# RetNet recurrence with a SwiGLU block: k's second layout made on TensorE for two chunks, q's decay table spread from two rows, four integer sums on GpSimd, and another order of the first steps

## The chip, the cores and the metric

The kernel runs on one core of a Trainium2 chip. The metric is the time of one execution in device microseconds (us). The core has TensorE (PE; PEld is its loading of weights), VectorE (DVE), ScalarE (ACT), GpSimd (POOL) and SyncE (SP), which here only issues DMA transfers. Each engine works through its own list of instructions in order and waits on semaphores for the others.

## The reference

```python
batch, n_heads, seq, head_dim = (4, 8, 768, 64)
gamma = 1.0 - 2.0 ** (-5.0 - np.arange(H))
for t in range(S):
    state = gamma * state + np.einsum('bhd,bhe->bhde', k[:, :, t], v[:, :, t])
    y[:, :, t] = scale * np.einsum('bhd,bhde->bhe', q[:, :, t], state)
x = y.transpose(0, 2, 1, 3).reshape(B * S, H * D)      # 3072 tokens x 512
g = x @ w_gate                                         # 512 x 1536
out = (g / (1 + np.exp(-g)) * (x @ w_val)) @ w_out     # 1536 x 512
```

q, k and v are float32. The three weights are float64, which the kernel reads as pairs of 32-bit words.

## The kernel before

**The work.** The sequence is cut into chunks of 128 steps, six for each of the four batch entries. Within a chunk the recurrence is a masked product: scores of k and q (`scores`, L628), times a decay mask on VectorE (L634), times v (`mix`, L713). From chunk to chunk a state of 64x64 a head is carried: `state` (L684) adds k scaled by its decay times v, `decay` (L670) shrinks the old one, and `mix_old` (L699) adds q, scaled by its own decay, times the state. The result x goes through the two weights (`plain_part` L906, `plain` L888, in later segments `product` L1057) and the third (`down`, L1126). Products of the second part are done with each operand split into three parts, made by ScalarE, VectorE and GpSimd in turn.

**Segments.** Six chunks make a segment (768 tokens), and there are four. The first segment's chunks 0 to 5 are handled one after the other at the start of the program, while the weights are read from HBM for the first time and turned from float64 into float32; only this start differs between the two kernels.

**The order** is written out by hand in the string `PLAN`. Of each entry the letter is the step, the number the chunk or piece, and what follows a colon a part of it: `s` scores, `m` mix, `o` mix_old, `t` state, `g` decay of the state, `x` splitting the result into parts (L969, L976, L399), `k`/`K` scaling k on GpSimd or VectorE (L649), `q`/`Q` scaling q (L643), `l3:1` loading for chunk 3 its piece 1 (pieces are k^T, q^T, v, k; called k, q, v and k_n here), `A` loading a third of the table of decays, `U` and `V` loading a piece of weights, `a`, `b`, `c`, `S`, `C` converting it (ScalarE L532, L535, L538; VectorE L545; sum L553 or L555), `n` splitting a weight (L960, L963, L966), `p`, `v`, `u`, `y` the first plain products and what follows them, `T` and `Z` making sums of a weight and writing it back, `h` and `L` small tables for later. `run` issues them in this order, so PLAN fixes the order on every engine.

**Two layouts of k.** The scores take k with the 64 elements of a head down the partitions; the state takes it with the 128 steps down the partitions. Both are loaded from HBM (`l0:0` and `l0:3` for chunk 0), as arrays laid out beforehand.

**Tables.** `tab` holds for each partition the masks (1024 columns), q's decay (512 columns, `qdec`), k's decay (8 columns, `kdec`) and the state's (4 columns). It is loaded in three slices, `A0`, `A1` (the masks) and `A2` (all the rest).

**Weights in halves.** The first two pieces of the first weights are converted half by half (`a0:0`, `a0:1` and so on). The low word is scaled by ScalarE (L538), the sign bits by ScalarE and VectorE (L535, L545), and an integer sum of both closes it (L553 on VectorE). For pieces of the third weight that sum is on GpSimd (L555).

**DMA.** All loads at the start but two (q of chunks 0 and 1, issued by ScalarE) are issued by SyncE in order. Eight semaphores are used in turn for all of them, so a load is issued when the one eight before it has landed.

Of the kernel before, what the change touches and what calls it, by code (L numbers as in the profile page):

```python
# [14 lines left out]
AF = mybir.ActivationFunctionType  # L15
ALU = mybir.AluOpType

P = 128
# [32 lines left out]
    l0:0 l1:0 A0 A1 s0 U0:0 l0:2 l0:3 a0:1 s1 b0:1 A2 h0 S0:1 m0 K0 x0:2 c0:1 l2:0 x0:1 l2:1 l1:3  # L51
    C0:1 t0 l1:2 V0:0 l3:1 n0:0 s2 a0:0 Q2 l3:0 l2:3 n0:1 b0:0 S0:0 m1 k1 x1:1 x1:2 l2:2 c0:0 n0:2
    U1:1 C0:0 t1 o2 l3:3 g2 s3 n0:3 n0:4 l4:1 p0:0 m2 a1:1 x2:1 k2 q3 b1:1 l4:0 a1:0 x2:2 S1:1 l5:1
    l3:2 n0:5 c1:1 k3 t2 C1:1 o3 b1:0 l5:0 l4:2 g3 v0:0 s4 S1:0 t3 l5:2 c1:0 C1:0 U2:0 m3 s5 U12:3
    U3:1 q5 q4 u0:0 a2 o5 o4 T0:0 n1:0 m4 b2 y0:0 x3:1 x3:2 m5 T0:1 n1:1 n1:3 T0:2 S2 n1:2 p0:1 v0:1
    n1:4 T1:0 x4:1 u0:1 y0:1 a12 n1:5 x5:1 U4:0 T1:1 a3 p1:0 x4:2 u1:0 p1:1 x5:2 Z0 u1:1 T1:2 c12
    v1:0 U5:1 y1:0 v1:1 p0:2 Z1 l5:3 v0:2 c2 C2 b12 y1:1 p1:2 n2:0 a4 U6:0 u0:2 b3 n2:1 u1:2 v1:2
    S12 n2:3 L y0:2 S3 c3 n2:2 U13:2 G2:0 n2:4 T2:0 G2:1 C3 y1:2 T2:1 n3:0 b4 n2:5 n3:1 i2:0 i2:1
    T2:2 W2:0 j2:0 n3:2 W2:1 G3:1 n3:3 S4 C12 a5 Z2 j2:1 Z12 n3:4 c4 C4 U7:1 n3:5 T3:0 T3:1 c13 T3:2
    G3:0 n4:0 n4:1 b5 S5 n4:2 W3:0 n4:3 W3:1 i3:0 i3:1 n4:4 a13 a6 G4:1 c5 Z3 b13 G4:0 T4:0 U8:0 C5  # L60
    T4:1 j3:1 n4:5 b6 U14:3 W4:1 n5:0 T4:2 n5:1 i4:1 n5:2 n5:3 j3:0 S6 i4:0 a7 c6 n5:4 W4:0 T5:0 C6
    G5:1 Z4 T5:1 n6:0 U9:1 j4:0 n5:5 S13 G5:0 a8 b7 n6:3 T5:2 j4:1 n6:1 c14 C13 W5:1 S7 i5:1 Z5 n6:4
# [12 lines left out]
    1/y0.05 T10:1 1/was0.1 1/y0.15 1/y0.00 1/y0.14 0/d2.1 0/D1.4 1/y0.12 0/d2.2 0/D1.2 1/y0.13 0/W3
    Z17 0/D1.3 0/Z2 0/d3.0 0/D1.0 0/h2.2 0/h3.1 1/C0 0/W4 T10:2 0/h3.2 0/d3.1 0/h4.2 Z10 1/y0.16
    1/l7 1/y0.17 1/new0.1 1/sum0.0 0/D2.3 0/D2.1 1/y0.10 0/h5.0 1/begin 1/sum0.1 0/d3.2 0/h5.1
    1/y0.11 0/D2.5 1/sc1 0/D2.0 0/d4.0 1/was1.0 0/D2.4 0/d4.1 0/D3.4 1/l6 1/dec1.1 0/h5.2 1/dec1.0
    0/D2.2 1/x0.2.0 0/D3.1 1/q1.1 0/d4.2 0/W5 0/D3.5 1/x0.1.0 0/h6.0 1/k1.0 0/Z3 1/sum0.3 1/k1.1
    1/sum0.2 1/x0.2.1 0/D4.5 0/D3.2 0/D3.3 0/D3.0 1/q1.0 0/Z4 0/h6.1 0/D4.0 0/D4.4 1/x0.1.2 1/x0.1.1  # L80
    1/A1 1/x0.0.0 0/d5.0 1/x0.2.2 1/y1.00 0/h6.2 1/y1.06 1/x0.0.2 1/new1.0 0/D4.2 0/d5.1 0/d5.2
    0/D4.3 0/D4.1 1/y1.07 1/y1.01 0/W6 0/h7.0 1/B1 1/x0.0.1 1/y1.04 1/y1.12 0/h7.1 1/l9 0/d6.0
    0/D5.4 0/h8.0 0/d6.1 1/y1.02 0/D5.3 0/D5.2 0/W7 0/h8.1 1/y1.05 0/d6.2 1/l8 1/l11 0/Z5 1/y1.03
    1/was1.1 0/D5.5 1/C1 0/d7.0 1/y1.16 0/d7.1 0/D6.5 0/D5.0 1/y1.17 1/y1.15 1/new1.1 0/h7.2 1/y1.14
    1/y1.11 0/D5.1 1/y1.13 1/x1.2.0 0/D6.3 0/d7.2 0/D6.4 0/Z6 1/y1.10 0/D7.3 0/h9.0 1/sc2 0/h8.2
    1/x1.2.2 0/D6.2 1/q2.1 1/k2.1 0/D7.5 0/W8 1/sum1.0 0/D6.1 1/sum1.2 1/k2.0 0/D6.0 0/D7.1 1/x1.1.0
    0/h10.0 0/h9.1 0/d8.0 0/D7.2 1/dec2.0 1/l10 1/sum1.1 1/dec2.1 0/W9 1/x1.1.1 0/D7.0 0/d8.1
    1/x1.2.1 0/Z7 1/sum1.3 1/was2.0 1/q2.0 1/x1.0.0 1/x1.1.2 0/d9.0 0/D7.4 0/d8.2 0/h11.0 1/A2
    1/new2.0 0/D8.0 1/x1.0.1 0/h10.1 0/D8.3 0/D8.2 0/d9.1 1/L0 0/D8.1 1/y2.00 0/D8.4 1/B2 0/W10
    0/d9.2 1/y2.07 1/y2.05 0/d10.0 0/D8.5 0/h9.2 1/y2.02 0/h11.1 0/D9.3 1/y2.03 0/h10.2 1/y2.01  # L90
    0/D9.5 0/Z8 1/y2.04 1/y2.06 1/w0.0.0 0/D9.4 0/d10.1 0/h11.2 1/C2 1/y2.16 1/y2.14 0/W11 1/y2.12
    0/D9.1 1/y2.10 0/D9.2 1/L1 0/d10.2 0/D10.3 0/Z9 0/d11.0 1/y2.17 1/x1.0.2 1/y2.15 1/y2.13 0/D9.0
    1/L2 0/D10.4 0/D10.1 1/sum2.2 0/D10.2 0/D10.0 1/y2.11 0/d11.1 1/sum2.0 0/d11.2 1/x2.1.0 1/sum2.1
    1/x2.1.2 1/sum2.3 0/D11.1 0/Z11 1/w0.1.0 0/D11.0 1/x2.0.0 0/D11.3 0/D10.5 0/D11.4 1/w0.0.1
    0/D11.2 1/w0.0.2 1/w1.0.0 1/x2.1.1 1/x2.0.1 0/Z10 1/w1.0.1 0/e0 1/x2.0.2 1/w1.0.2 0/D11.5 1/p0.0
    1/u0.0 1/p0.1 1/p0.2 1/p1.0 1/x2.2.0 1/u0.1 1/w0.2.0 0/e2 1/x2.2.1 1/w0.1.1 1/p1.1 1/x2.2.2 0/e1
    1/w0.1.2 0/e3 1/w1.2.0 1/w1.1.0 1/w0.2.1 1/u1.0 1/w2.1.0 1/u0.3 1/p1.2 1/w1.1.1 1/p0.3 1/u0.4
    1/p0.4 1/w0.2.2 1/u0.5 1/p0.5 1/u0.6 1/w1.2.1 1/w2.0.0 1/w1.1.2 1/u1.3 1/p0.6 1/u0.8 1/p1.3
    1/w2.0.1 1/p1.4 1/u1.4 1/w2.0.2 1/u1.1 1/L3 1/u0.9 1/p1.5 1/p2.0 1/w2.2.0 1/w1.2.2 1/u1.5
    1/w3.2.0 1/u0.2 1/w2.1.1 1/w3.2.1 1/u1.2 1/w3.1.0 1/u1.6 1/u2.0 1/w3.0.0 1/w3.0.1 1/p1.6  # L100
    1/w2.1.2 1/p2.1 1/p2.3 1/w3.1.1 1/L4 1/p2.2 1/u1.8 1/u2.4 1/u2.1 1/u2.3 1/p2.5 1/w3.0.2 1/w4.2.0
    1/u1.9 1/u2.6 1/w2.2.1 1/p2.4 1/w3.2.2 1/L5 1/p3.1 1/w2.2.2 1/u2.5 1/u1.7 1/w4.1.0 1/w4.0.0
    1/u0.7 1/p3.0 1/u3.0 1/w3.1.2 1/w4.0.1 1/w4.1.1 1/p2.6 1/p3.2 1/u3.3 1/p3.3 1/p3.4 1/u3.4 1/u2.2
    1/u2.8 1/p3.5 1/u3.1 1/u3.5 1/L6 1/w5.1.0 1/p3.6 1/w4.0.2 1/u2.9 1/w4.1.2 1/u3.6 1/w5.0.0
    1/w4.2.1 1/p4.1 1/w5.0.1 1/p4.0 0/e5 2/begin 1/w5.2.0 1/w5.0.2 1/u3.8 1/p4.3 1/u4.0 1/w5.1.1
    1/u4.4 1/u3.9 1/w5.2.1 1/p4.2 1/u4.3 1/L7 1/u3.2 1/w5.1.2 1/p4.5 1/p5.0 1/u4.1 1/p4.4 1/u4.5
    1/w6.1.0 1/p5.1 1/u5.0 1/w4.2.2 1/w6.0.0 1/w6.1.1 1/p5.2 1/u5.1 1/u4.6 0/e4 1/w6.1.2 1/u2.7
    1/w6.0.1 1/w6.2.0 1/w5.2.2 1/u5.3 1/p4.6 1/p5.3 1/p5.4 1/u5.4 1/u4.8 1/p5.5 1/u5.5 1/L8 1/w7.2.0
    1/p5.6 1/u4.9 1/w6.0.2 1/u4.2 1/w7.1.0 1/w8.2.0 1/p6.1 1/u5.6 1/w7.0.0 1/u4.7 1/w7.2.1 1/p6.0
    1/u3.7 1/w7.1.1 1/w7.0.1 1/u6.0 1/w8.2.1 1/u5.2 1/u6.1 1/L10 1/p6.3 1/w7.0.2 1/u6.4 1/u5.8  # L110
# [1198 lines left out]
```

## Time and profile before

| what | value |
|---|---|
| median of three runs | 642.8 us (642.61 to 645.92) |
| the profiled execution | 642.91 us |
| its span, first to last instruction | 641.1 us |
| TensorE busy | 631.2 us, 98% |
| DMA share in 24.18:32.02 us | 1.06 of 16 engines, 373 GB/s |

The page's slices show how TensorE and the DMA engines are filled over the span, each digit a fortieth (16 us) and in tenths:

```profile
PE   6999999999999999999999999999999999999997
...
DMA  9998978689887445258775540467777444304554
```

Reading: TensorE is short of work in the first slice and at the very end only. The chain that ended last runs over TensorE for 94% of the span and over DMA transfers for 4%:

```profile
PE 94%; DMA 4%; ACT 0%; DVE 0%; SPq 0%; issue 0%; ACTq 0%
```

### The profile page before, as it was taken

What the parts mean: (1) busy time and instruction counts of PE and PEld (TensorE: products, weight loads), DVE (VectorE), ACT (ScalarE), POOL (GpSimd) and SP (SyncE); (2) the same over time, 40 slices, a digit from 0 to 9 for tenths busy, and PEclk for the clock granted to TensorE, in tenths of its full rate; (3) what the DMA queues carried; (4) which work ended last, traced back from release to release, by engine and by line L of the source; (5) the groups of instructions that cost most, each with busy time, mean ns of one, the idle gap of its engine ahead of it and who ended that gap; (6) DMA issues with size and microseconds to landing.
All of it is one profiled execution on the core that took longest, in us unless ns stands there. A gap on an engine that the chain in (4) does not pass through costs nothing.

```text
span 641.1 us, 14110 instructions
## 1 busy us (share of the span) xinstructions
PE 631.2 (98%) x5579; PEld 579.5 (90%) x5579; DVE 485.6 (76%) x713; ACT 392.2 (61%) x860; POOL 265.4 (41%) x174
## 2 busy tenths in 40 slices
PE   6999999999999999999999999999999999999997
PEld 6899999988779999997778999998777999999886
DVE  5887888999898887665787869675789866768351
ACT  3687697777865565566766555564785555654221
POOL 0535455544427865630002665550101666663000
PEclk9999999999999999999999999999999999999999
DMA  9998978689887445258775540467777444304554
GB/s 322 375 359 295 356 264 301 267 306 319 269 278 290 168 148 173 73 180 260 246 240 214 199 160 10 183 196 243 228 240 263 157 164 172 116 0 153 193 184 178
DMA packets 50626, 140.13 MB, mean 219 GB/s; under 512 B 4992, under 2 KB 17792, under 8 KB 50560
## 3 DMA queue, kind: packets, MB, share of 16 engines
q1 hardware_dynamic: 49984, 138.44, 62.8%
q8 instruction: 44, 0.72, 0.5%
q10 hardware_dynamic: 576, 0.79, 0.3%
q14 instruction: 22, 0.18, 0.1%
HBM read 109.32 MB, written 29.88 MB: 217 GB/s over the span
## 4 chain that ended last, share of the span: by engine, by line
PE 94%; DMA 4%; ACT 0%; DVE 0%; SPq 0%; issue 0%; ACTq 0%
PE bank L1057 41%; PE bank L1126 31%; PE bank L888 13%; PE bank L758 6%; PE bank L906 2%; DMA rawp<-in_w_gate_dram 1%; DMA oitem<-wdnt 1%; DMA hT<-in_k_n_dram 1%; DMA hT<-in_q_t_dram 1%; PE bank L713 0%; PE bank L684 0%; PE bank L699 0%; PE bank L628 0%; SPq L464 0%; DVE bank L545 0%
## 5 line engine op out<-in xcount | busy, mean ns | idle before, releaser
L1126 PE MATMUL bank<-oitem,gitem 128*128 128x512 f32 x867 | 208.4, 394 | 0.5 <-DMA oitem<-wdnt 0.3
L1126 PEld LDWEIGHTS bank<-oitem,gitem 128*128 128x128 f32 x867 | 159.6, 188 | 35.2 <-DMA oitem<-wdnt 0.7
L966 POOL TENSOR_TENSOR gitem<-gitem 128x768 fp32r<-128x768 f32 x72 | 142.0, 1982 | 115.3 <-DVE gitem L963 96.3
L1057 PE MATMUL bank<-xa,gitem 128*128 128x384 f32 x864 | 160.5, 334 | 0.0
L1057 PEld LDWEIGHTS bank<-xa,gitem 128*128 128x128 f32 x864 | 150.8, 188 | 0.2
L966 POOL TENSOR_TENSOR oitem<-oitem 128x256 fp32r<-128x256 f32 (+1 forms) x60 | 65.9, 1106 | 53.7 <-DVE oitem L963 53.3
L1057 PE MATMUL bank<-xb,gitem 128*128 128x384 f32 x432 | 84.5, 334 | 0.0
L888 PE MATMUL bank<-xa,oitem 128*128 128x384 f32 x480 | 84.2, 335 | 0.0
L963 DVE SCALAR_TENSOR_TENSOR gitem<-gitem,loads 128x768 fp32r<-128x768 f32 x72 | 76.0, 1070 | 9.9 <-ACT gitem L960 8.4
L888 PEld LDWEIGHTS bank<-xa,oitem 128*128 128x128 f32 x480 | 83.0, 188 | 0.2
L1057 PEld LDWEIGHTS bank<-xb,gitem 128*128 128x128 f32 x432 | 75.9, 188 | 0.4
L960 ACT ACTIVATE gitem<-loads 128x768 fp32r<-128x768 f32 x72 | 59.6, 843 | 26.0 <-PE bank L1057 16.8
L963 DVE SCALAR_TENSOR_TENSOR gitem<-gitem,hT 128x768 fp32r<-128x768 f32 x48 | 46.2, 965 | 26.1 <-ACT gitem L960 26.1
L960 ACT ACTIVATE gitem<-hT 128x768 fp32r<-128x768 f32 x48 | 40.2, 842 | 32.8 <-PE bank L1126 30.7
L991 ACT COPY chunk_x<-bank 64x128 f32<-64x128 f32 x144 | 36.6, 260 | 31.8 <-PE bank L758 21.2
L399 DVE SCALAR_TENSOR_TENSOR gitem<-gitem 128x768 fp32r<-128x768 f32 x48 | 48.8, 1025 | 0.8
L785 POOL TENSOR_TENSOR loads<-loads,tab 128x512 f32<-128x512 f32 x9 | 13.3, 1479 | 81.8 <-PE bank L758 58.4
L1057 PE MATMUL bank<-xb,oitem 128*128 128x384 f32 x216 | 43.4, 335 | 0.0
L1057 PEld LDWEIGHTS bank<-xb,oitem 128*128 128x128 f32 x216 | 37.9, 188 | 0.3
L1074 DVE TENSOR_TENSOR hT<-bank,tmp 128x384 f32<-128x384 f32 x36 | 20.0, 555 | 20.4 <-PE bank L1057 20.2
L1072 ACT COPY tmp<-bank 128x384 f32<-128x384 f32 x36 | 17.2, 478 | 28.3 <-PE bank L1057 19.3
L963 DVE SCALAR_TENSOR_TENSOR oitem<-oitem,loads 128x256 fp32r<-128x256 f32 (+1 forms) x42 | 33.8, 808 | 0.9 <-ACT oitem L960 0.8
(114 smaller groups left out, 785.7 us busy)
## 6 DMA issues: line engine op xcount, KB each, us to landing
loads<-wup SPq DMA_DIRECT2D x36, 896.0 KB, 4.6
oitem<-wdnt SPq DMA_DIRECT2D x33, 768.0 KB, 4.4
wdnt<-oitem SPq DMA_DIRECT2D x12, 768.0 KB, 6.1
wup<-first SPq DMA_DIRECT2D x9, 896.0 KB, 6.0
rawp<-in_w_gate_dram SPq DMA_DIRECT2D x12, 512.0 KB, 7.2
rawp<-in_w_val_dram SPq DMA_DIRECT2D x12, 512.0 KB, 6.3
rawp<-in_w_out_dram SPq DMA_DIRECT2D x12, 512.0 KB, 7.3
out_dram<-chunk_x SPq DMA_DIRECT2D x21, 256.0 KB, 2.2
```

The costliest lines, as they stand in the source:

```text
L399: stt(o, x, 1.0, y, op0=mul, op1=op)
L758: nc.tensor.matmul(o, a, b, start=start, stop=True, skip_group_check=True)
L785: (pool if i else both)(t, t, qdec, op=mul)
L888: nc.tensor.matmul(o, w[:, a, ts(b, P)], X0[:, a, i, NC - 1 - b], start=a == b == 0, stop=a == 2 and b == NC - 1, skip_group_check=True)
L960: act(o[0], x, AF.Copy, scale=CUT / FAR)
L963: stt(o[1], f32(o[0]), -FAR, x, op0=mul, op1=add)
L966: op(o[2], f32(o[0]), f32(o[1]), op=add)
L991: copy(cx[half[i], ds(2 * h, 2), c, half[z]], y.rearrange("p (b t) -> p b t", b=2))
L1057: nc.tensor.matmul(o, w[:, a, k], x[:, a, KH - 1 - k], start=start and a == k == 0, stop=a == 2 and k == KH - 1, skip_group_check=True)
L1072: steps = (lambda: copy(p1, x), lambda: tt(c11, z, p1, op=add), lambda: act(gate, c11, AF.Silu, scale=ONE), lambda: copy(u2, x), lambda: c ...
L1074: lambda: copy(p5, wb), lambda: tt(h1, x, p5, op=add),
L1126: nc.tensor.matmul(banks[tok][:, cols], hs[f][:, a, ds(i * TH + u * P, P)], wo[f][:, a, cols], start=f == a == 0, stop=f == NF - 1 and a = ...
```

## The change

Eight things are other than before, all in the start:

- k_n of chunks 0 and 1 is not loaded (`l0:3`, `l1:3` gone). `r0` and `r1` make it on TensorE: k^T of each pair of heads is taken as weights against a unit matrix (`unit_of`, step `I`, made of the mask's diagonal on VectorE), four matmuls 128x128 by 128 columns into bank 2 or 3.
- k of chunk 0 is scaled on VectorE as before (`K0`), now from bank 2; k of chunk 1 by ScalarE in eight pieces from bank 3 (`E1`), no longer by GpSimd (`k1`).
- q's decay table is not loaded whole. `R` loads two rows of it (one for each half of the partitions), `D` spreads them with two matmuls against a row of ones into bank 2, `F` copies the bank to `tab` on ScalarE.
- `B` loads the 12 columns of small tables that were in `A2`, by themselves.
- The four half pieces of the first weights get their integer sum on GpSimd (128x512 each); the bit step writes over the piece, not into a bank, and the scaled low word is written over the raw words.
- v of chunk 0 is loaded ahead of the first weight piece, v of chunk 1 and the second half of that weight earlier.
- The steps of the first third of PLAN stand in another order; from "T11:2 n11:5 c17" on it is the same.
- `w` is a new name for a warming matmul that PLAN does not use.

On TensorE the first steps stood `s0 s1 m0 t0 s2 m1 t1 o2 s3 p0:0 m2 t2 o3 v0:0 s4 t3 m3 s5 o5 o4 m5 m4`. Now they stand `D s0 s1 m0 r0 r1 s2 t0 m1 o2 t1 s3 o3 m2 t2 s4 p0:0 v0:0 m3 t3 s5 o5 o4 m5 m4`, and the other plain products follow in both.

```diff
-    l0:0 l1:0 A0 A1 s0 U0:0 l0:2 l0:3 a0:1 s1 b0:1 A2 h0 S0:1 m0 K0 x0:2 c0:1 l2:0 x0:1 l2:1 l1:3
-    C0:1 t0 l1:2 V0:0 l3:1 n0:0 s2 a0:0 Q2 l3:0 l2:3 n0:1 b0:0 S0:0 m1 k1 x1:1 x1:2 l2:2 c0:0 n0:2
...
+    l0:0 R0 A0 D0 l1:0 I0 A1 F0 l0:2 h0 U0:0 a0:1 s0 s1 l2:0 m0 b0:1 B0 l2:1 l1:2 r0 c0:1 r1 K0 S0:1
+    E1 V0:0 l3:1 s2 C0:1 l3:0 t0 Q2 x0:2 a0:0 m1 x1:2 n0:0 l2:3 l2:2 o2 n0:1 b0:0 t1 S0:0 c0:0 l4:1
...
-                to = d if piece[0] == "up" else lo
+                to = d if piece[0] == "up" and half is None else lo
...
-                stt(o if piece[0] == "up" else u[:, cols], u[:, cols], 3, o,
+                stt(o if piece[0] == "up" and half is None else u[:, cols], u[:, cols], 3, o,
...
-            if piece[0] == "up":
+            if piece[0] == "up" and half is None:
                 tt(d, signs_of(piece, half)[0][0].bitcast(I32), d, op=add)
             else:
                 pool(d, d, lo, op=add)
...
+    def scale_k_act(c):
+        kd, src = (t.rearrange("p (h d) -> p h d", h=H)
+                   for t in (chunks[c][3], turned.pop(c, chunks[c][3])))
+        for h in range(H):
+            act(kd[:, h], src[:, h], AF.Copy, scale=kdec[:, ds(h, 1)])
...
+    def unit_of():
+        nc.vector.tensor_scalar(unit, mask[:, 0, 0], 0.124, None, op0=ALU.is_ge)
...
+    two_rows = loads[0:1, ds(0, 2 * NP * P)]
+    ones = loads[0:1, ds(2 * NP * P, D)]
+
+    def small_tables():
+        nc.sync.dma_start(out=tab[:, KDEC0:NTAB], in_=decays[:, KDEC0:NTAB])
+
+    def decay_rows():
+        for i in range(2):
+            nc.sync.dma_start(out=two_rows[:, ts(i, NP * P)],
+                              in_=decays[ds(D * i, 1), QDEC0:KDEC0])
+
+    def spread_rows():
+        nc.vector.memset(ones, 1.0)
+        for i in range(2):
+            nc.tensor.matmul(banks[2][ds(D * i, D)], ones, two_rows[:, ts(i, NP * P)],
+                             start=True, stop=True, skip_group_check=True)
+
+    def keep_rows():
+        copy(tab[:, QDEC0:KDEC0], banks[2])
...
     def rows_of(n):
...
-        if not turned:
-            nc.vector.tensor_scalar(unit, mask[:, 0, 0], 0.124, None, op0=ALU.is_ge)
         kt, t = pairs(chunks[c][0]), banks[2 + n]
         for m in range(NP):
             nc.tensor.matmul(t[:, ts(m, P)], kt[:, m], unit, start=(m == 0), stop=True,
                              skip_group_check=True)
```

## The prediction

> **What bounds the kernel now.** I read the page's busy times first, then the busy time by stretches, then who waited for whom on TensorE, then the order of time of the first 32 us.
>
> ```profile
> span 641.1 us, 14110 instructions
> PE 631.2 (98%) x5579; PEld 579.5 (90%) x5579; DVE 485.6 (76%) x713; ACT 392.2 (61%) x860; POOL 265.4 (41%) x174
> ```
>
> TensorE is busy for 631.2 of 641.1 us, so all that can be won without taking work from it is 9.9 us. The stretches say where these lie (the columns after the length are PE, PEld, DVE, ACT, POOL, clock, DMA share, GB/s):
>
> ```profile
> 4.90:7.30 2.40, 2.35 (x32) 2.17 (x32) 0.46 (x1) 0.00 (x0) 0.00 (x0) 1.00 1.03 379
> 7.30:9.75 2.45, 0.00 (x1) 0.03 (x1) 2.06 (x4) 0.76 (x2) 0.00 (x0) 1.00 1.07 387
> ...
> 15.59:24.18 8.59, 7.94 (x104) 7.10 (x105) 6.92 (x12) 6.37 (x15) 5.85 (x5) 1.00 1.08 376
> 24.18:32.02 7.84, 7.54 (x128) 6.74 (x128) 7.00 (x14) 5.10 (x11) 2.51 (x2) 1.00 1.06 373
> 32.02:45.24 13.22, 13.22 (x112) 13.22 (x111) 11.80 (x22) 11.75 (x18) 4.52 (x3) 1.00 1.05 363
> ```
>
> From 32.02 us on TensorE is full; before that it has holes, while the DMA engines are full (share 1.03 to 1.08). The waits on TensorE between 4.9 and 32 us:
>
> ```profile
> PE bank L713 <- DMA hT<-in_v_n_dram: 2.5, 1, 2.5
> PE bank L684 <- DVE hT L649: 1.0, 1, 1.0
> PE bank L628 <- DMA hT<-in_k_t_dram: 0.6, 1, 0.6
> PE bank L699 <- DVE loads L643: 0.3, 1, 0.3
> PE bank L684 <- DVE first L553: 0.3, 1, 0.3
> ```
>
> That is 4.7 us; a small one makes it 4.8. The rest of the 9.9 us is the first 1.1 us and the way out of the last result, which the change does not touch. So the change is decided in the first 32 us: TensorE reaches its full stretch at 32.02 us, and every us by which that moves moves the end.
>
> **Prices.** Start to start in order of time:
>
> ```profile
> 13.73 1.09 PE L713 MATMUL bank<-tmp,hT 128*64 128x128 f32 x16
> ...
> 14.65 0.64 PE L684 MATMUL bank<-hT 128*64 128x64 f32 x16
> ...
> 16.61 1.16 PE L628 MATMUL bank<-hT 64*128 64x128 f32 x16
> ...
> 17.70 1.70 PE L906 MATMUL bank<-xa,oitem 128*128 128x256 f32 x12
> ```
>
> A mix (m, L713) takes 0.92 us, a scores step (s, L628) 1.09, and from the same view a state step (t) 0.56, a mix with the old state (o) 1.02, twelve plain matmuls (L906) 1.63.
>
> **The change, part by part.**
>
> *Bytes.* Gone are k_n of chunks 0 and 1 (2 x 262,144 B) and the third table slice (128 x 524 x 4 = 268,288 B). Added are two rows (4,096 B) and the small tables (6,144 B). Net 782,336 B; at 376 GB/s (stretches above) 2.1 us less transfer ahead of all later loads. SyncE's issues stay equal in number, three for three. The two row issues stand ahead of the masks (A0, A1) and of k of chunk 1; at 0.45 us an issue these are issued 0.9 to 1.3 us later. It costs nothing: the queue has q and k of the first chunks to move meanwhile (the second mask is the sixth big load before and after, landing near 7.5 us). If that cover went, the masks' first use on VectorE would be late by up to 0.9 us.
>
> *v of chunk 0 moves ahead of the first weight piece.* That piece is 524,288 B, 1.4 us at that rate, so v lands near 8.2 instead of 9.6 us. The 2.5 us wait is then set by VectorE: the masking of the first scores, two instructions of 0.68 us behind s0.
>
> *TensorE makes k's rows (r0, r1).* Each is four f32 matmuls 128x128 by 128 columns. No row has this at the later pace. Below: if they went like L713's half-wide ones, 4 x 0.92 / 8 = 0.46 us. Above: the opening group L1222 has just this shape, 8 in 3.78 us, so 1.89 us. I take 0.92: L713's matmuls go in pairs side by side, so eight of them are four full-wide ones. Both: 1.85 us (0.9 to 3.8).
>
> *TensorE spreads the table (D).* Two matmuls of 64x512 columns from one row, on both halves of the columns. Below: L713's pair takes 0.23 us for 128 columns, four times that is 0.92; were the two records of an f32 matmul as quick as L1126's 512 columns (394 ns busy, some 0.24 from start to start) 0.5. Above: at the opening group's pace and not side by side, 3.8. The pace itself changes just there: between 4.94 and 5.62 us TensorE shows 6 records of L628, in the next 0.68 us 16.
>
> ```profile
> 4.94:5.62 0.68, 0.68 (x6) 1.00 1.00 368
> 5.62:6.30 0.68, 0.68 (x16) 1.00 1.00 380
> ```
>
> So D, starting at 4.95 when the rows have landed behind k and q of chunk 0, runs 0.65 us slow and the rest quick: 1.2 us. s0 then comes wholly in the quick time and is 0.4 us shorter; D costs 0.8 net.
>
> (The Trainium skill, "TensorE: Matmul & The Clock Gate", Part 1, says that the array starts at half clock and goes to full after about 3.4 us of sustained work, in a window that does not start with the kernel. The jump at 5.6 us agrees, though the clock column shows 1.00 throughout. By the rule the jump could come one window later; that is the third rival.)
>
> *VectorE* loses the sum of the four half pieces (L553, 4 x 0.69 = 2.75 us) and gains a unit matrix and a memset, 0.2 us each from the 0.19 us row of L1237. K0 now waits for r0; behind it stand the first weight's bit step and the next masks. By the walk below r0 ends at 10.4, and those need the weight piece (9.6) plus two ACT steps anyway.
>
> *ScalarE* gains the copy of the table (0.6, as L738's 0.61) and k of chunk 1 in eight pieces of 128x64 (E: L793's 32 such pieces take 7.9 us, so 2.0). Behind E stands the copy of the first state, which o2 on TensorE needs: this is the new wait.
>
> *GpSimd* gains four integer sums of 128x512: half of L555's 2572 ns for 1024, 1.29 us each, 5.1 in all; it loses chunk 1's k (1.04). Its busy time in the first 32 us is 9.60, so there is room. Ahead of q5, for o5, it has the first two sums.
>
> **The walk on TensorE.** D 4.95 to 6.15; s0, s1 to 7.95 (0.9 each at 16 records per 0.68 and a little fill); m0 waits for two masks until 8.6 and ends at 9.5; r0, r1 to 11.4; s2 (q lands near 11.1) to 12.5; t0 to 13.05; m1 to 13.97. ScalarE: weight piece at 9.6, its three steps and one for x (0.6 each) to 12.05, E to 14.0, state copy to 14.4, so o2 waits 0.4 and ends at 15.4. Then t1, s3, o3, m2, t2, s4 to 20.65, two plain groups to 23.95, m3, t3, s5 to 26.5, o5 and o4 (28.23 to 30.12 before: 1.89) to 28.4, m5, m4 to 30.3. The last load, v of chunk 5, was issued at 22.03 and landed 5.4 us later, 27.4; 2.1 earlier it is no limit. GpSimd has q5 at about 25.7 against o5 at 26.5. That is 1.7 us ahead of 32.02.
>
> The other way round: 4.8 us of waits go, 1.85 and 0.8 of work and 1.05 of new waits (0.65 + 0.4) come: 1.1 ahead. The two differ by fills that the first counts too tightly. I take 1.3 us. The profiled execution took 642.9 us (span 641.1 and 1.8 around it), the median is 642.8; less 1.3 that is 641.5.
>
> **Rivals.**
>
> 1. *Nothing is left of it*: GpSimd sets the pace. For it: VectorE's L399 at 128x256 takes 412 ns quiet and 769 in its "loads" form, with GpSimd at work. If the sums take a whole 2.57 us, q5 comes at 26.8 and o5 waits 0.4; if 3.5 us, some 2 us are lost over o5 and the first plain groups. Against: L643, L649 and L966 ran at their shortest (1.04 to 1.30) up to 32 us. Time 641.9 to 643.5. (The Trainium skill, "GPSIMD Engine Reference", Key points, warns of the interface shared with VectorE, for instructions with two SBUF inputs; it would put the loss here too.)
>
> 2. *More is gained*: D at 0.5, r at half of my price, both new waits gone: 1.3 + 0.7 + 0.9 + 0.6 would be 3.5. As a step that comes early soon waits for the next, I count half of the extra 2.2: 2.4 gained, 640.5. For it: every load is 2 us early. Against: the masks stay on VectorE.
>
> 3. *The slow pace lasts one window longer*, from 5.6 to 9.0 us, because D waits for its rows or uses one row only. Then s0, s1 and m0 go at half pace: 3.4 us of time do the work of 1.7, and the masks slide with s0, so no wait takes it up: 1.7 lost. Time 641.5 + 1.7 = 643.2, slower than before. It decides if the records of s0 come at 0.2 us a pair.
>
> 4. *A stall past the start*: the sums of the second piece put GpSimd's third parts for p1:0 late (needed near 33 us, ready near 32 by the walk). One us of slack; with rival 3 or slow sums together the loss reaches 4 to 5 us: 646 to 647.
>
> **How the numbers follow.** Forecast 0.50 (640.6 to 642.4 as its own range), rival 1 0.13, rival 2 0.10, rival 3 0.11, rival 4 0.16. Low 639.9 is 3.0 of rival 2's 3.5; high 644.6 is rival 3 with most of rival 1's 2 us. They leave out rival 4 and the far end of 2. A difference of 0.5%, 3.2 us, is about what a measurement of this kernel tells from none. Faster by that needs nearly all of rival 2, half of its chance: 0.05. Slower: rival 4, and 0.01 for 1 and 3 together: 0.17. Within: 0.78.
>
> **What would show it.** Right: no wait on v of chunk 0; TensorE's waits from 5 to 32 us below 1.5 us in all, named VectorE's masks and ScalarE's state copy; L692's eight matmuls near 1.9 us and L681 near 1.2; the last mix ending and the full stretch starting between 30.2 and 31.4 us; after that as many waits as before (0.5 us). Wrong: L555 over 2 us at 128x512 with "POOL" named on L729 or L936; slow records past 5.7 us; any wait over 0.3 us between 32 and 130 us; or a full stretch beginning at 32 us or later.

## The result, and the profile after

| | before | changed |
|---|---|---|
| median, 13 runs each | 644.32 us (642.61 to 648.74) | 646.99 us (643.34 to 648.74) |
| the profiled execution | 642.91 us | 647.43 us |
| its span | 641.1 us | 644.9 us |

The ratio is 1.0041, with an interval of 1.0023 to 1.0058: the change costs 0.4%, some 2.6 us, where 1.3 us of gain was forecast. The forecast was wrong in its sign, and the median lies outside its range.

The page of the changed kernel, its first lines:

```profile
span 644.9 us, 14171 instructions
PE 636.9 (99%) x5599; PEld 583.0 (90%) x5599; DVE 484.4 (75%) x711; ACT 394.7 (61%) x869; POOL 269.0 (42%) x177
```

TensorE is busy for 636.9 us instead of 631.2. The idle time did shrink, from 9.9 to 8.0 us, but 5.7 us of busy time came in, with 20 more matmuls. The busy time by stretches of the changed kernel (columns after the length: PE, PEld, DVE, ACT, POOL, clock, DMA share, GB/s):

```profile
4.90:7.30 2.40, 2.40 (x6) 0.79 (x8) 0.23 (x1) 0.24 (x1) 0.00 (x0) 1.00 1.00 371
7.30:9.75 2.45, 2.45 (x26) 2.45 (x26) 0.68 (x2) 0.96 (x2) 0.00 (x0) 1.00 0.93 292
...
15.59:24.18 8.59, 7.26 (x125) 6.32 (x122) 8.29 (x13) 6.70 (x19) 5.86 (x5) 1.00 1.07 373
24.18:32.02 7.84, 7.84 (x117) 7.35 (x117) 6.99 (x13) 4.43 (x8) 6.51 (x6) 1.00 0.79 274
32.02:45.24 13.22, 13.22 (x124) 13.05 (x119) 9.21 (x17) 8.60 (x12) 2.59 (x2) 1.00 0.82 270
```

The hole of 7.30 to 9.75 is filled (2.45 busy, it was 0.00), but between 4.90 and 9.75 us TensorE got through 32 matmul records in 4.85 us, as many as in the 2.40 us of the first of these stretches before. It is busy, but at half pace. The order of time shows which work that is:

```profile
4.80 2.22 PE L681 MATMUL bank<-loads 1*64 1x512 f32 x4
6.95 3.38 PE L631 MATMUL bank<-hT 64*128 64x128 f32 x32
10.26 1.25 PE L743 MATMUL bank<-tmp,hT 128*64 128x128 f32 x16
11.44 2.05 PE L692 MATMUL bank<-loads,hT 128*128 128x128 f32 x16
```

The spreading (D, L681) takes 2.15 us to the next start and the two scores 3.31; the trace's record of the clock steps to full at 9.77 us, where before it did at 5.59. The waits of the changed kernel on TensorE, over the whole span but for its first 1.1 us:

```profile
PE bank L729 <- DVE loads L646: 1.3, 1, 1.3
PE bank L788 <- issue: 1.2, 1, 1.2
...
PE bank L1156 <- DVE hT L442: 0.4, 1, 0.4
PE bank L1156 <- DMA oitem<-wdnt: 0.3, 1, 0.3
PE bank L918 <- DVE hT L442: 0.2, 1, 0.2
```

The first is at 17.40 us (o2). All others lie past 88 us, where TensorE does the same work in the same order in both kernels, and the largest of them waits for nothing that the profile can name. (TensorE's order is the same from 27.1 us of the kernel before and 28.3 us of the changed one on. VectorE's and ScalarE's are not: in the traces they come together only at 131 and 125 us of the changed kernel, so more than the first 32 us differs.) Against before, the first of the second products (L918, L888 before) starts 1.14 us later (47.66 for 46.52 us), at 78 us it is still 1.14, at 110 us 1.97, at the first product of the third weight (L1156) 2.52, 40 matmuls on 3.87, and 3.82 at the end.

### The profile page after: what moved, and what is told of

Same layout as the page of the kernel before. It is cut to its first block, busy times and chain, and to the rows that moved or that the text cites. A ratio compares the mean times of both kernels' runs of the same rounds, so it can differ in the third digit from the quotient of the medians.

```text
span 644.9 us, 14171 instructions
## 1 busy us (share of the span) xinstructions
PE 636.9 (99%) x5599; PEld 583.0 (90%) x5599; DVE 484.4 (75%) x711; ACT 394.7 (61%) x869; POOL 269.0 (42%) x177
## 4 chain that ended last, share of the span: by engine, by line
PE 88%; DMA 5%; DVE 2%; ACT 2%; issue 2%; SPq 1%; ACTq 0%; DVEq 0%
PE bank L1087 41%; PE bank L1156 31%; PE bank L788 6%; PE bank L918 5%; PE bank L631 1%; DMA wup<-loads 1%; DMA wdn<-first 1%; DMA rawp<-in_w_gate_dram 1%; DMA rawp<-in_w_out_dram 1%; DMA oitem<-wdnt 1%; PE bank L743 1%; PE bank L936 1%; ACT first L532 1%; PE bank L729 1%; PE bank L1252 1%
## 5 line engine op out<-in xcount | busy, mean ns | idle before, releaser
L1156 PE MATMUL bank<-oitem,gitem 128*128 128x512 f32 x867 | 208.2, 394 | 0.7 <-DVE hT L442 0.4
L1156 PEld LDWEIGHTS bank<-oitem,gitem 128*128 128x128 f32 x867 | 159.6, 188 | 35.3 <-DMA oitem<-wdnt 0.8
L918 PE MATMUL bank<-xa,oitem 128*128 128x384 f32 x480 | 84.7, 336 | 0.2 <-DVE hT L442 0.2
L993 DVE SCALAR_TENSOR_TENSOR gitem<-gitem,loads 128x768 fp32r<-128x768 f32 x72 | 77.5, 1090 | 9.4 <-ACT gitem L990 8.0
L996 POOL TENSOR_TENSOR oitem<-oitem 128x256 fp32r<-128x256 f32 (+1 forms) x60 | 63.9, 1072 | 48.6 <-DVE oitem L993 44.7
L918 PEld LDWEIGHTS bank<-xa,oitem 128*128 128x128 f32 x480 | 83.0, 188 | 1.1 <-DVE hT L442 0.5
```

The lines of the kernel that those rows point to most:

```text
L918: nc.tensor.matmul(o, w[:, a, ts(b, P)], X0[:, a, i, NC - 1 - b], start=a == b == 0, stop=a == 2 and b == NC - 1, skip_group_check=True)
L993: stt(o[1], f32(o[0]), -FAR, x, op0=mul, op1=add)
L996: op(o[2], f32(o[0]), f32(o[1]), op=add)
L1156: nc.tensor.matmul(banks[tok][:, cols], hs[f][:, a, ds(i * TH + u * P, P)], wo[f][:, a, cols], start=f == a == 0, stop=f == NF - 1 and a = ...
```

## The experiments

All ratios are to the kernel before, run beside each on the same chip. The table has what the text reads from it: when the clock record goes to full, when the first second product starts, and the wait named "issue" on L788 near 141 us (L758 in the kernel before).

| run | edit | full clock, us | second products, us | wait L788, us | ratio, interval |
|---|---|---|---|---|---|
| before | | 5.59 | 46.52 | none | 1 |
| changed | | 9.77 | 47.66 | 1.24 | 1.0041, 1.0023 to 1.0058 |
| e1 | D behind the scores | 7.12 | 45.82 | 1.09 | 1.0027, 1.0015 to 1.0038 |
| e2 | a2 earlier | 13.17 | 49.03 | 1.32 | 1.0046, 1.0027 to 1.0065 |
| e3 | sums on VectorE | 4.16 | 50.32 | 1.22 | 1.0114, 1.0094 to 1.0135 |
| e4 | table loaded whole | 4.71 | 44.91 | none | 0.9995, 0.9983 to 1.0008 |
| f1 | e1, 16 fewer | 6.77 | 48.90 | none | 1.003, 1.001 to 1.005 |
| f2 | e4, 16 more | 5.22 | 45.24 | none | 1.0002, 0.9991 to 1.0014 |
| f3 | changed, 16 fewer | 4.90 | 45.38 | none | 1.0008, 0.9992 to 1.0024 |
| f4 | before, 40 more | 8.16 | 46.86 | 1.23 | 1.0019, 1.0006 to 1.0033 |
| g1 | f3, D over all rows | 6.30 | 46.61 | none | 1.0003, 0.9989 to 1.0016 |
| g2 | f3 again | 5.12 | 46.00 | none | 1.0016, 0.9994 to 1.0038 |
| g3 | f3, sums on VectorE | 5.12 | 49.13 | none | 1.0064, 1.004 to 1.0088 |
| g4 | e4, 16 fewer | 4.67 | 45.00 | none | 0.999, 0.9977 to 1.0003 |
| h1 | changed again | 10.34 | 47.60 | 1.36 | 1.0045, 1.0025 to 1.0066 |
| h2 | f3 again | 5.19 | 46.18 | none | 1.0015, 0.9999 to 1.0032 |
| h3 | e1 again | 4.33 | 46.61 | 0.95 | 1.0027, 1.0014 to 1.004 |
| h4 | f1 again | 4.31 | 46.62 | none | 1.0023, 1.0004 to 1.0042 |

In f1, f4 and e3 the clock fell back for one window of 3.41 to 3.42 us soon after it had opened, in e2 once at 204.31 us. "16 fewer" and the like count TensorE's instructions ahead of the same work. In e3 and g3 part of the first weights is summed from other words than the reference's; the amount of work is that of the old three steps. Lines of PLAN are shown in part.

**First four: the clock, the weight stream, the sums, the table.** In e1 the spreading stands behind the first scores (the memset of the ones with it):

```diff
-    l0:0 R0 A0 D0 l1:0 I0 A1 F0 l0:2 h0 U0:0 a0:1 s0 s1 l2:0 m0 b0:1 B0
+    l0:0 R0 A0 l1:0 I0 A1 l0:2 h0 U0:0 s0 s1 D0 F0 a0:1 l2:0 m0 b0:1 B0
```

> The table is spread (D, F) after s0 and s1 on TensorE instead of before them, with the row of ones set earlier; all else as in the changed kernel. Theory 1 (the clock): D's thin matmuls do not keep TensorE's clock opening on time, so the quick pace came at 9.8 us instead of 5.6. Then here the quick pace comes between 4.5 and 8 us, D takes 0.9 to 1.2 us instead of 2.15, and the third group of plain matmuls starts at 31.0 to 32.2 us instead of 33.16; time 1 to 2 us below the changed kernel. Rival (the added work alone is the loss, the clock's opening is chance): D 0.9 to 1.2 us, s0 and s1 as slow as in the changed kernel in half of such runs, start of the third group 32.2 us or later.

It took 645.45 us, and the start came as theory 1 expected (clock at 7.12 us, third plain group at 31.32 us). In its profile D takes 1.07 us, the second products start 0.70 us ahead of before, and yet the end is 1.6 us behind: the start is not the whole loss. The two waits past 130 us are there again, 0.6 and 1.1 us.

In e2 ScalarE's first step for the third weight piece stands ahead of the last mix of the start, so that SyncE's next loads go out earlier:

```diff
-    T0:1 T0:2 x4:2 y0:0 u0:1 n1:5 T1:0 p1:0 a2 U4:0 y0:1
+    T0:1 T0:2 x4:2 y0:0 u0:1 n1:5 T1:0 p1:0 U4:0 y0:1
...
-    o5 m4 n1:3
+    o5 a2 m4 n1:3
```

> The first conversion step of the third weight piece (a2 on ScalarE) stands ahead of m4 instead of behind u0:1; all else as in the changed kernel. Theory 2 (the weight stream): the waits of TensorE after 90 us (2.7 us more than before in all) come from a2, which waits behind u0:1 for the plain products, so that the load U4:0 is issued at 36.35 instead of 31.75 us. Then here U4:0 is issued at 31 to 32.5 us, the waits on VectorE's hT at 94 and 135 us go, the start of the third group stays at 33.2 +- 0.5, and the time is 1.5 to 2.7 us below the changed kernel. Rival (the four sums on GpSimd hold the stream, by the release of the raw words for U3:1): U4:0 earlier, but waits of 1 us or more stay past 90 us and the time moves by less than 1 us.

646.15 us: no gain that shows. The weight piece was issued 4.15 us earlier against the third plain group, and both late waits stayed (0.6 and 1.3 us). The 0.8 us that the changed kernel lost between 78 and 110 us isn't here, but neither is it in h1, the changed kernel itself: it belongs to that one execution. The stream of weights is not the cause. Its clock opened last of all, at 13.17 us.

In e3 the four integer sums are VectorE's again:

```diff
-                to = d if piece[0] == "up" and half is None else lo
+                to = d if piece[0] == "up" else lo
...
-            if piece[0] == "up" and half is None:
+            if piece[0] == "up":
```

> The four integer sums are on VectorE again, by the old three lines; order and all else as in the changed kernel. Theory 3 (GpSimd): with the sum gone from GpSimd, its q3 does not run beside VectorE's Q2 (1.43 us there, 0.68 before), the wait of 1.3 us at o2 goes, U3:1 is issued 2 to 3 us earlier than 30.8, and the time is 1 to 3 us below the changed kernel. By theories 1 and 2 alone: o2's wait shrinks by up to 1.3 us, the waits past 90 us stay, the time moves by 0 to 1 us.

651.48 us, 4.5 us over the changed kernel's median, where every theory had expected about the same or less. g3 repeats it below on a better base. In e4 the table is loaded as before, with no rows, no spreading and no copy:

```diff
-    l0:0 R0 A0 D0 l1:0 I0 A1 F0 l0:2 h0 U0:0 a0:1 s0 s1 l2:0 m0 b0:1 B0
+    l0:0 A0 l1:0 I0 A1 l0:2 h0 U0:0 a0:1 s0 s1 l2:0 m0 b0:1 A2
```

> The third slice of the table is loaded whole again (268 KB at the place of the small tables) and nothing is spread; rows of k still made on TensorE, order and sums as in the changed kernel. Theory 1: s0 follows the warming matmuls at 4.9 us, quick pace from 4.5 to 8 us, 2.15 us of TensorE work and 1 us of slow pace gone; start of the third group 30.5 to 32 us, time 1.5 to 3 us below the changed kernel, unless the loads, 0.7 us later each, set the pace. Rival (bytes decide): start of the third group within 0.5 us of 33.2.

643.16 us, as before, and both late waits are gone. So the spreading brings the loss, and part of it comes 130 us later. Taking 2.2 us of work away can't do that by itself: the waits come or go where the programs are equal.

**Why TensorE waits at 141 us.** The order of time of the changed kernel there:

```profile
139.45 1.67 PE L1156 MATMUL bank<-oitem,gitem 128*128 128x512 f32 x6
141.05 0.46 PE L788 MATMUL bank<-loads,states 64*64 64x64 f32 x16
141.34 0.65 PE L788 MATMUL bank<-tmp,loads 64*64 64x64 f32 x32
141.80 0.41 PE L788 MATMUL bank<-loads,states 64*64 64x64 f32 x14
143.44 0.27 PE L788 MATMUL bank<-loads,states 64*64 64x64 f32 x2 [1.24 <-issue]
```

A group of 16 equal matmuls stops after 14 of them, waiting for no engine. What does arrive there is in the view of DMA queues for 138.4 to 143.5 us:

```profile
q1 hardware_dynamic: 498, 1.85, 92.1%
q8 instruction: 1, 0.02, 1.1%
```

Queue q8 carries instructions. In the whole span it has 44 pieces of 16,384 B, and TensorE has 11,282 instructions in the trace (weight loads, matmuls and the few others): some 256 a piece. In every one of the seven profiles with this wait, the instruction that waits has 2,497 (in f4 2,498) of TensorE's before it, which is 9 x 256 + 193 (194); the same kind of wait at 181 to 187 us, 0.07 to 0.37 us in before, f3, g4, h1 and h4, falls on 14 x 256 + 193 or 194. And it ends 2.2 to 2.5 us after a piece begins on q8. So TensorE stands at the end of a block of 256 instructions whose successor isn't there yet. In the changed kernel the piece began 2.67 us after TensorE had entered the last block it had, and TensorE ran through that block's 256 instructions in 3.8 us, as the many small matmuls of L788 fall into it. In the seven profiles the piece began 2.4 to 2.8 us into the block.

(The Trainium skill, "Runtime: NRT & Kernel Launch", Instruction fetch mechanics, says that each engine's instructions are brought in blocks of 256 by a DMA queue of its own while the present ones run, and that this is mostly hidden. The block size agrees; the 1.24 us here were not hidden.)

f1 is e1, f2 is e4, f3 the changed kernel and f4 the kernel before with another number of instructions in the warm-up ahead of everything, where TensorE waits for loads anyway. In f1 and f3:

```diff
-            nc.tensor.matmul(banks[3][:, :P], warm[:, :P], warm[:, :P], start=True, stop=True,
+            nc.tensor.matmul(banks[3][:, : 2 * P].rearrange("p (a b) -> p a b", a=2), warm[:, :P],
+                             warm[:, None, :P].to_broadcast([P, 2, P]), start=True, stop=True,
...
-    warm_up(8)
+    warm_up(4)
```

> The kernel of e1 with four warm-up matmuls of 256 columns instead of eight of 128: the same columns, 16 TensorE instructions fewer ahead of everything else. In the four profiles with the spread table the 16 KB piece of instructions that the trace shows on DMA queue q8 begins 92.1 to 94.4 us after the third plain group (L936), on top of the loads of the first output words, and one of the sixteen parts of these loads lands 1.25 us after the other fifteen; in the two profiles without the table it begins at 95.7 to 95.8, behind them. Theory A (the fetch of instructions): q8 sends 256 of TensorE's instructions at a time, so the number of instructions ahead decides where it falls; with 16 fewer it falls at about 95.8, the waits of 0.6 and 1.1 us at about 132 and 141 us are gone, and the time is 1.7 us under e1's, that is 1.000 of the kernel before (0.998 to 1.002). Theory B (the order of the loads, or the table's own work): the fetch has nothing to do with it, both waits stay, and the time stays at 1.0027.

> The changed kernel itself with four warm-up matmuls of 256 columns instead of eight of 128. Theory A: no waits of 0.4 and 1.2 us at about 135 and 143 us, and the ratio goes from 1.0041 to about 1.0015. Theory B: both stay, 1.004. It is also one more look at when the quick pace begins with the spreading matmuls (L681) first: by the theory that these four, with one row each, don't count as work for the clock, at 9.5 us or later as in the changed kernel (9.77) and e2 (13.17); by the rival that the moment is as good as chance, anywhere from 4 to 10 us as in e3 (4.16).

In f2 and f4 `warm_up` takes a width w for both operands:

```diff
-    warm_up(8)
+    warm_up(8, 64)
+    warm_up(4)
```

```diff
-    warm_up(8)
+    warm_up(15, 16)
+    warm_up(3)
```

> The kernel of e4 (q's decay loaded whole) with eight warm-up matmuls of 64 columns and four of 128 instead of eight of 128: the same columns, 16 TensorE instructions more, which is 7 more than in the kernel of e1 by this point. Theory A: the fetch on q8 falls at about 92 us after the third plain group, the waits of about 0.6 and 1.1 us come up at about 132 and 140 us though there is no spread table, and the time is 1.002 of the kernel before (0.9995 plus 1.7 us). Theory B: no such waits, 0.9995 as e4.

> The kernel before, with nothing changed but the warm-up: fifteen matmuls of 16 columns and three of 128 instead of eight of 128, which makes 40 TensorE instructions more, as many as the changed kernel has. Theory A: the fetch on q8 falls on the first output words, and waits of 0.4 to 0.6 and 1.1 to 1.3 us come up at about 131 and 139 us; 1.7 us or 1.003 by this alone. The small warm-ups may also let the quick pace begin later than 5.6 us; what that costs is then read from the start of the third plain group, 32.0 us in the kernel before. Theory B: no waits there.

The kernel before with 40 instructions more has the wait at the same matmul, the 15th of the same group:

```profile
139.76 0.41 PE L758 MATMUL bank<-loads,states 64*64 64x64 f32 x14
141.40 0.33 PE L758 MATMUL bank<-loads,states 64*64 64x64 f32 x2 [1.23 <-issue]
```

and costs 1.0019, that is 1.2 us, with nothing changed but the warm-up (in the profile 0.34 us of it are lost by the third plain group already). The changed kernel with 16 fewer has lost it in f3, g2 and h2; h2's group runs through:

```profile
138.45 0.46 PE L788 MATMUL bank<-loads,states 64*64 64x64 f32 x16
138.74 0.65 PE L788 MATMUL bank<-tmp,loads 64*64 64x64 f32 x32
139.20 0.41 PE L788 MATMUL bank<-loads,states 64*64 64x64 f32 x16
```

This shows the cause of the wait at 141 us. Why 16 fewer are enough can be read from the trace: with the spreading in the kernel, the block that ends near there is then cut elsewhere and takes 5.1 us instead of 3.8, and a piece that begins 1.4 to 2.5 us into it (f1, f3, g1, g2, g3, h2, h4) is in time.

What was expected of the wait at 132 us (L1156 <- DVE hT L442) holds less well. It was put down to the piece on q8 that falls on the loads of the first output words: one of a load's sixteen parts then lands late (e2: fifteen by 2.97 us after the issue, the sixteenth at 4.24). That part of it holds: in the six profiles in which the piece began 0.7 to 1.0 us after the issue of this load (oitem<-wdn, L1132; e1, e2, e3, f2, h1, h3) the last part landed 0.7 to 1.9 us behind the fifteenth, in the other twelve at most 0.4. The wait on TensorE was there in six of the seven profiles in which the piece began within 2.4 us of that issue, 0.4 to 1.1 us, but also in three of the eleven in which it began later (f1 0.5, f3 0.3, g1 0.9). So these waits have another cause beside it, which is open. VectorE's and ScalarE's other order before 131 us is a candidate that wasn't tried: the two profiles with the old order (before, f4) have no such wait, but their piece began late as well. f2 missed on its wait near 140 us: 7 instructions further on the piece began 1.42 us after the block's entry instead of 2.67, and TensorE just didn't run dry. What sets that delay wasn't tried. f1 missed on time, which h4 takes up.

**Does one row count for the clock?** g1 is f3 with

```diff
-            nc.tensor.matmul(banks[2][ds(D * i, D)], ones, two_rows[:, ts(i, NP * P)],
-                             start=True, stop=True, skip_group_check=True)
+            nc.tensor.matmul(banks[2][ds(D * i, D)].rearrange("p (a b) -> p a b", a=4), warm[:, :D],
+                             warm[:, None, :P].to_broadcast([P, 4, P]),
+                             start=True, stop=True, skip_group_check=True)
```

> The kernel of f3 with the two spreading matmuls over all 128 rows instead of one (zeros times zeros, so the table of q's decay is left zero); their shape to TensorE's output, their passes and the number of instructions are the same. Theory (clock by windows): the clock record changes only at steps of 3.41 us whose phase is the run's own; a window in which TensorE worked about 82% or more opens the next one, and matmuls with one row don't count as work: in the profiles so far every window of 83% and more opened the quick pace, while the windows with the spreading in them (6.36 in the changed kernel, 6.34 and 9.75 in e2) did not. So here the quick pace begins by 7.4 us whatever the phase, the spreading costs its own time alone, and the time is 0.5 to 1.3 us under f3's, with less scatter. Rival (the moment is chance, rows don't matter): the same distribution as g2, quick pace at up to 10 us or later.

and g2 is its control:

> The kernel of f3 once more, as the control of g1, g3 and g4 on the same chip. By the theory of windows the quick pace begins between 3.9 and 5.4 us in some 45 of 100 executions (1.52 of the 3.41 us of possible phases) and at 8.8 us or later in the others. No wait of about 1.2 us at about 140 us (TensorE's instructions arriving late), whatever the clock did; ratio 1.0008 as f3, within its interval of 0.9992 to 1.0024.

f3 itself had missed what was expected of its clock: it opened at 4.90 us, not at 9.5 or later. The window before that, 1.49 to 4.90 us, was full of warm-up matmuls, as the spreading began only at 4.79; this is where the phase of the windows came in. In g1 the clock opened at 6.30 us, while the spreading over all rows still ran (4.79 to 6.60 us):

```profile
4.79 1.81 PE L681 MATMUL bank<-warm 128*64 128x512 f32 x4
6.53 2.06 PE L631 MATMUL bank<-hT 64*128 64x128 f32 x32
```

The scores take 2.0 us there, 3.3 in the changed kernel, whose window ended at nearly the same place (6.36 us) without opening. Taking windows of 3.41 us back from each opening, in all 18 profiles: with one-row matmuls counted as idle, every window with 83% of work or more opened the clock, and none with 81% or less. (The two that set these figures, the changed kernel's to 9.77 and e2's to 9.76 us, differ by 0.05 us of work, so the level hangs on one window each.) Counted as work, four windows that were full did not open it (the changed kernel's to 6.36, e2's to 6.34 and 9.76, h1's to 6.93 us; 56, 57, 81 and 46% without the one-row matmuls). So one row does not count. Closing fits this too: at 38 to 41% of work in a window the clock fell back (f4, f1, e3), at 46% once (e2, to 204.31 us) and once not (e3, to 34.88 us), and at 50 to 53% it stayed (before, h3, g1); f1's window has 67% if its one-row matmuls count. In time, g1's median is 643.77 us against g2's 644.70, but the intervals overlap; from the lowest to the highest time g1 spans 2.9 us and g2 6.1, the smaller scatter that was expected. f1 shows the clock closing by the same rule (clock is the column before the DMA share), after a wait of 1.1 us for k of chunk 1 and the spreading in one window:

```profile
3.36:6.77 3.41, 3.41 (x20) 2.45 (x18) 0.00 (x0) 0.00 (x0) 0.00 (x0) 1.00 0.96 325
6.77:10.19 3.42, 2.30 (x24) 1.29 (x24) 2.50 (x5) 0.62 (x1) 0.00 (x0) 1.00 1.02 356
10.19:13.60 3.41, 3.41 (x24) 3.08 (x24) 0.26 (x1) 2.70 (x5) 0.00 (x0) 0.50 1.07 377
13.60:17.01 3.41, 3.41 (x56) 3.17 (x57) 2.38 (x4) 2.32 (x11) 1.60 (x2) 1.00 1.05 381
```

24 records in the window at 0.50, 56 in the next. The 1.00 of the first line is wrong: the record has no entry before the first step, and the 20 records in it are the slow pace. The same goes for the 1.00 that the prediction's stretches show ahead of 5.59 us.

(The Trainium skill, "TensorE: Matmul & The Clock Gate", Part 1, gives a free-running window of about 3.4 us; the steps of 3.41 and 3.42 us agree.)

**The sums.** g3 is f3 with e3's lines, and the sign step ahead of the low word's:

```diff
-    r0 c0:1 r1 K0 S0:1
+    r0 r1 K0 S0:1 c0:1
...
-    b1:1 c1:1 S1:1 q4
+    b1:1 S1:1 c1:1 q4
```

> The kernel of f3 with the four integer sums of the first words back on VectorE, in the old three steps, with the sign step ahead of the low word's step as those need it. Theory that GpSimd's sums set the pace (they hold back its q3 and, by the shared port, VectorE's Q2 of 1.43 us, which TensorE waits for at o2): the wait at o2 (0.6 to 1.3 us) goes, and the time is 0.5 to 1.0 us under g2's. Theory that VectorE is the tighter of the two: its 1.4 us of old steps come back in the same stretch, new waits of 1 us or more on VectorE's first words come up between 15 and 35 us, and the time is 1 us or more above g2's.

647.65 us, some 3 over g2 beside it. Its waits on TensorE from 2 to 36 us:

```profile
PE bank L729 <- DVE loads L646: 2.2, 1, 2.2
PE bank L743 <- DVE first L553: 1.9, 1, 1.9
```

VectorE is the tighter of the two; GpSimd's sums are a gain. The wait at o2, which they were suspected of, grows without them.

**A version to keep.** g4 is e4 with the warm-up of f1:

> The kernel of e4 (q's decay loaded whole, no spreading) with four warm-up matmuls of 256 columns: the version that should do best. By the block theory the boundary of a block of 256 TensorE instructions falls 16 later in the kernel than in e4, the stretch of 13.60 us that begins at the first L1156 group's first matmul becomes 13.15 as in f1 and f3, and nothing is waited for at 140 us: 0.9990 of the kernel before (0.998 to 1.000). By the rival that alignment only moves waits about, 0.9995 as e4.

643.34 us, 0.999 of before: the stretch from the first L1156 over 40 matmuls took 13.19 us (13.60 in e4, 14.68 in the changed kernel). It is below the changed kernel by about 0.5%, but its interval still touches 1, so no version was shown to beat the kernel before.

**Two by two.** The changed kernel, f3, e1 and f1 once more on one chip:

> The changed kernel once more, beside h2 (16 TensorE instructions fewer), h3 (the spreading behind the first scores) and h4 (both). By the theory of instruction blocks the wait on L788 of 1.1 to 1.3 us at about 143 us is in this profile whatever its start looks like, since it follows from the program alone; ratio 1.004 (1.002 to 1.006).

> As f3 and g2: no wait on L788 at about 140 us; 1.0012 (their mean), 1.2 us or more under h1. If alignment isn't worth its wait, within 0.5 us of h1.

> As e1: the wait on L788 of 1.1 us is there; 1.0027. By the theory of clock windows it begins quick by 7.4 us in every execution, so it has less scatter than h1 and is up to 1.5 us under it; if rows don't matter to the clock, as h1.

> As f1, whose 1.003 missed what was forecast for it: no wait on L788. By the theory that f1's time was a chance draw of late starts (its profile had one more window of 3.41 us at half pace), 1.2 us under h3, 1.000 to 1.002; if it stays at 1.003, something in this order costs 1 us at its start in most executions, and the profile's first 20 us show what.

| median, us | as many instructions | 16 fewer |
|---|---|---|
| spreading first | h1 646.25 | h2 643.90 |
| behind the scores | h3 645.32 | h4 643.76 |

With 16 fewer, 2.4 and 1.6 us go by the medians; the wait itself was 1.36 and 0.95. By the ratios it is 1.9 and 0.3 us, and of h3 and h4 the intervals overlap widely, so behind the scores the gain isn't shown. The waits from 130 to 190 us in h1 (h2 has none over 0.15 us):

```profile
PE bank L788 <- issue: 1.7, 2, 1.4
PE bank L1156 <- DVE hT L442: 1.1, 1, 1.1
```

By place of the spreading 0.9 us go with as many instructions and 0.1 with fewer; by ratios the second is even a loss (1.0015 to 1.0023, intervals overlapping). h4's median does what was expected of it (its ratio doesn't quite), but two of its twelve executions took 648 to 649 us. From lowest to highest h3 spans 2.6 us against h1's 5.4, as expected, but h4 6.3 against h2's 5.0. h4's profile says why later isn't better: waits for loads that the spreading hid, 0.9 us for k of chunk 1 and 0.3 for q of chunk 0, come out. (The longer wait for q, 0.9 us for chunk 2, h2 has too.)

```profile
PE bank L631 <- DMA hT<-in_q_t_dram: 1.2, 2, 0.9
PE bank L631 <- DMA hT<-in_k_t_dram: 0.9, 1, 0.9
PE bank L729 <- ACT first L532: 0.6, 1, 0.6
```

and such a wait in the wrong window closes the clock, as in f1. That this made the two long ones is likely, and not shown.

## Why the prediction was wrong

Its profiled time was to be 641.5 and was 647.4 us, 5.9 more. (The kernel before, taken as 642.8 us from three runs, has a median of 644.32 over thirteen; the ratios beside each other don't hang on that.) The full stretch (third plain group) began at 33.16 instead of 30.7: 2.46. From there to the end 2.68 were lost: 0.83 between 78 and 110 us, which h1, the same kernel, doesn't show, and the rest in the waits at 135 and 143 us with what they pull along. What lies around the span was 2.5 us, taken as 1.8.

- *"After that as many waits as before (0.5)"* is the first of two steps that failed, and the one that no rival had. The sum took everything past 45 us as equal, because TensorE's program is. TensorE's work is equal there, but starts 39 of its instructions later (8 of the spreading, 32 of r0 and r1, one other thing fewer), and the blocks of 256 are cut elsewhere: 1.24 us. Rival 4 had a stall past the start, but at GpSimd's parts; no wait on GpSimd came.
- *D at 1.2 us, "0.65 us slow and the rest quick"*: 2.15, and the scores behind it slow as well, until 9.77 us. This is the second step that failed. It is rival 3, given 0.11, by its own second reason (one row only), and with its own sign of records at 0.2 us a pair. Its price of 1.7 us is near what the opening cost: with the clock open as D begins (f3, g2, h2: 4.9 to 5.2 us) the second products start 0.3 to 1.1 us ahead of before, with it late (changed, h1) 1.1 behind.
- *Waits of 4.8 us go*: right, the hole is filled; the new wait at o2 was 1.33 where 0.4 was taken, and on VectorE's Q2, which took 1.43 us instead of 0.68 beside GpSimd's q3, not on ScalarE's state copy. m0 did not wait, as the scores were late. Q2's time goes with which of the two begins first: in the eight profiles in which GpSimd's q3 did, Q2 took 1.36 to 1.77 us and o2 waited 1.3 to 2.2; in the eight in which Q2 did, 0.68 and 0.6. The two in the changed kernel (start and length in us first):

```profile
15.43 1.28 POOL L646 TENSOR_TENSOR loads<-hT,tab 128x512 f32<-128x512 f32 x1
...
15.83 1.43 DVE L646 TENSOR_TENSOR loads<-hT,tab 128x512 f32<-128x512 f32 x1
```

- *r0 and r1 at 1.85*: 1.98. *GpSimd's sums at 1.29*: four at 1.30 on average. Both right, by L713's price and by the half of L555's.
- *Rival 1, GpSimd sets the pace*: fell; moving the sums back costs some 3 us. *Rival 2*, more gained: it needed D at 0.5, and D took 1.0 at its best (e1, to the next start).
- The chances gave slower by over 0.5% 0.17 and within 0.78; at 0.41% the case is the middle one, at the wrong side of it.

So some 1.2 of the 2.6 us are the wait at the end of a block of instructions itself. By the ratios (changed and h1, 1.0043, against f3, g2 and h2, 1.0013) 1.9 us go with 16 fewer and 0.8 are left, but the 1.9 hold more than that wait: the one at 132 to 135 us shrinks with it, and in the profiles with the spreading first the clock opened at 4.9 to 5.2 us with 16 fewer (f3, g2, g3, h2) and at 9.8 to 13.2 us in three of four with as many (changed, e2, h1; e3 at 4.16). Whether that is chance or comes from the other warm-up isn't shown. The 0.8 that are left are put down to starts that open late, by the theory of windows in some 55 of 100 executions (expectation of g2). At 0.3 to 1.1 us gained and 1.1 lost, half of each makes only some 0.2 us, so this part is not shown: late starts would have to be more frequent or cost more. How often it opens late the executions without a profile can't show.

## What to carry to other kernels

Where a later part of the program waits for "issue" and its code was not touched, look at the queue that carries instructions and count the engine's instructions: a few more or fewer at the very start, in a warm-up, move the wait or take it away. Ahead of the clock's opening put matmuls over all rows, not thin ones; behind the opening a thin one costs its own time, as in e1, unless the window has too little other work: f1's, at 40%, closed the clock. And an edit that fills a wait for loads is worth what the next wait behind it leaves.

## What was not expected of the hardware

- TensorE runs dry at the end of a block of 256 instructions (0.95 to 1.36 us at one place in seven profiles), when it passes a block in 3.8 us and the next begins to arrive 2.4 to 2.8 us into it; 2.2 to 2.5 us pass from that to the next matmul.
- Matmuls over one row are not work to the clock: four full windows of 3.41 us with them did not open it, one with the same shape over 128 rows did.
- The clock goes back to half for a whole window of 3.41 us with 38 to 41% of work in the window before (f1's 2.30 us of 3.42 are 40% without the one-row matmuls); at 46% it did once and once not, at 50% and more it didn't.
- With a piece of instructions beginning 0.7 to 1.0 us after a load's issue, one of the load's sixteen parts landed 0.7 to 1.9 us behind the others (six of six profiles; at most 0.4 in the other twelve), and its reader waits for that part (in e1 ScalarE's L999 begins 0.08 us after it).
- VectorE's 128x512 multiply of two operands took 0.68 us when it began ahead of GpSimd's of the same shape, and 1.36 to 1.77 us when it began behind it (eight profiles each).
